# The last tile's stores, one transfer a quadrant instead of two, and another order of the last products, in a linear-attention and mixture-of-experts kernel

## The chip, the cores and the metric

The kernel runs on one core of a Trainium2 chip. The metric is the device time of one execution in microseconds (us); for several runs it is their median. A core has five engines with instruction streams of their own, which wait for each other through semaphores: TensorE (PE, its weight loads are shown as PEld), VectorE (DVE), ScalarE (ACT), GpSimd (POOL) and SyncE (SP). Transfers (DMAs) are issued by SP, ACT or POOL and carried out by 16 DMA engines.

## What is computed

```
x   = linear attention of q, k, v          # 8 batches, 8 heads, 576 positions, 64 wide
x   = x as 4608 tokens of 512              # token = batch * 576 + position
p   = domain_probs / (sum + 1e-9)          # 4608 x 4
out = 0
for e in range(4):                         # four experts
    h = max(x @ w1[e], 0)                  # 512 -> 1024
    out += p[:, e:e+1] * (h @ w2[e])       # 1024 -> 512
```

The output is 4608 x 512 in float32.

## The kernel before

**Tiles.** The tokens are worked on in nine tiles of 512 (`NT`). Tiles 0 to 7 are the first 512 positions of the eight batches. Tile 8, the last, collects the 64 positions that are left over in each batch (512 to 575). A tile has four subtiles `ns` of 128 tokens, one to a partition; in tile 8 a subtile is two batches of 64 positions: batch 2·ns on partitions 0 to 63, batch 2·ns+1 on partitions 64 to 127. In the output these two pieces lie 576 rows apart.

**Products.** For each tile but the first and each expert (a unit, 32 of them) both layers multiply two by two blocks with seven products instead of eight. Layer 1 is done by `Block` in two halves (`d` = 0, 1) and leaves the hidden values `h`; POOL forms four sums of them a half (`hidden_sum`, L776 to L782), each of 128 x 512 elements. Layer 2 (`layer2_product`, L784) has products numbered 1 to 7, each for two token groups `i` = 0, 1. One of them is four matmuls (L809) of 128 x 256 into half a PSUM bank, after which VectorE adds the bank, times p, to the float32 accumulator of the subtile (`add_acc`, L705). Products 1, 6, 7 and 4 run on in one bank half (`run`), so 4 can only start when the accumulation of 7 has read it; 2, 5 and 3 use the other (`side`). A name such as m83.41 is tile 8, expert 3, product 4, group 1. Two units follow each other at the end: m82.* and, behind it, m83.*, the last. In the last unit `run` and `side` are banks of their own (pb, pe) instead of halves of py.

**Order.** The order of work is written by hand. Every piece has a position (a number); `work` is sorted by it (L1100) and then issued one after the other (L1115), which sets the order on every engine. Layer 2's products of a unit stand at `at` + `L2AT[m]`, in the order `L2ORD`, (2, 5, 1, 6, 3, 7, 4); the last unit has an order of its own and stands 7 later (L1075). A piece that yields is driven to its end before the next one begins, so a product, its accumulation and its store are recorded together.

**Stores.** `store` (L683) writes an accumulator to the output. For tiles 0 to 7 that is one transfer on SP of 128 rows of 2,048 bytes (256 KB, L686). For tile 8 it writes only a quadrant at a time, 128 rows of 256 columns (1,024 bytes): two transfers of 64 rows, one per batch, on SP and ACT (L692). Products 2, 3, 4 and 7 each finish a quadrant per group, so there are eight quadrants and 16 transfers of 64 KB. Those of product 7, group 1, are both on POOL (L832). A transfer raises one semaphore when it lands; eight semaphores (lanes) serve SP's and ACT's transfers in turn, and a transfer first waits until the former one of its lane has landed. Behind the last instruction, SP tests the lanes one after the other (L1143), and a barrier of all engines ends the execution.

Of the kernel before, what the change touches and what calls it, by code (L numbers as in the profile page):

```python
# [80 lines left out]
    "KC": ('VV', 'VA', 'AA', 'AV'),  # L81
    "XT": ('AA', 'VV', 'VA', 'VV'),
    "CUT": (((0, 3, 4), (0, 3, 4), (0, 4), (0, 4)), ((0, 2, 4),) * 4),
    "WARM": (14, 5, 3, 1, 2, 1, 1),
    "BANK": {'qT0': 'b', 'qT1': 'py', 'kv2': 'py', 'qT2': 'py', 'kv3': 'b', 'nd10': 'b', 'nd10+': 'py', 'nd00': 'py', 'xT20': 'b', 'nd01': 'b', 'xT00': 'b', 'xT10': 'py', 'xT30': 'py', 'nd11': 'b', 'L20': 'b', 'xT11': 'b', 'L30': 'e', 'L10': 'e', 'L11': 'e', 'L00': 'py', 'L31': 'b', 'L01': 'e', 'L21': 'py', 'b1.lk': 'py', 'b1.q1': 'py', 'b1.q3': 'b', 'b1.q0': 'py', 'b1.nd10': 'b', 'b1.qT0': 'py', 'b1.nd00': 'b', 'b1.xT0': 'b', 'b1.xT3': 'py', 'b1.qTl': 'py', 'b1.nl': 'py'},
    "EARLY": (
# [36 lines left out]
def kernel(  # L123
# [10 lines left out]
    nc = tc.nc  # L134
    ATTN, HSUM, L2ORD, L2AT = (CFG[x] for x in ("ATTN", "HSUM", "L2ORD", "L2AT"))

    B, H, S, D = q.shape
    N, E = moe_domain_probs.shape
    _, Dm, F = moe_w1.shape

    P = 128
    HP = P // 2
    CM = S // P
    SM = CM * P
# [67 lines left out]
    out_b = out.rearrange("(b s) d -> b s d", s=S)  # L212
# [467 lines left out]
    def new_py():  # L680
        return ppm.tile([P, Dm], FP32, tag="py", bufs=2, name="py")

    def store(j, ns, cols=slice(0, Dm), engs=(nc.sync, nc.scalar)):  # L683
        acc = accs[j, ns][:, cols]
        if j < B:
            nc.sync.dma_start(  # L686
                out=out_b[j, 0:SM].rearrange("(p c) d -> c p d", c=CM)[ns],
                in_=acc,
            )
        else:  # L690
            for u in range(2):
                engs[u].dma_start(  # L692
                    out=out_b[2 * ns + u, SM:S, cols],
                    in_=acc[u * HP : (u + 1) * HP],
                )

    def add_acc(j, e, ns, ps, ds, first):
        if (j, ns) not in accs:
            accs[j, ns] = pm.tile([P, Dm], FP32, tag="acc", bufs=NACC, name="acc")
        acc = accs[j, ns][:, ds]  # L700
        pscal = p_sb[:, j, ns, e : e + 1]
        if first:
            nc.scalar.activation(acc, ps, AF.Identity, scale=pscal)  # L703
        else:
            nc.vector.scalar_tensor_tensor(  # L705
                out=acc, in0=ps, scalar=pscal, in1=acc, op0=AO.mult, op1=AO.add
            )
# [61 lines left out]
    def hidden_sum(h, hs, i):  # L769

        a11, a21 = h[:, :, 0, 0:NH], h[:, :, 0, NH:NT]
        a12, a22 = h[:, :, 1, 0:NH], h[:, :, 1, NH:NT]
        if i != 2:
            hs[i] = pm.tile([P, 2, NH], FP16, tag=f"hs{i}", bufs=2, name=f"hs{i}")
        if i == 0:
            nc.gpsimd.tensor_tensor(out=hs[0], in0=a21, in1=a22, op=AO.add)  # L776
        elif i == 1:
            nc.gpsimd.tensor_tensor(out=hs[1], in0=hs[0], in1=a11, op=AO.subtract)  # L778
        elif i == 2:
            nc.gpsimd.tensor_tensor(out=a21, in0=a11, in1=a21, op=AO.subtract)  # L780
        else:
            nc.gpsimd.tensor_tensor(out=hs[3], in0=a12, in1=hs[1], op=AO.subtract)  # L782

    def layer2_product(j, e, hT, hss, p, i):  # L784


        if (j, e) == (NTILES - 1, E - 1):
            if p == 1:
                pys[j, e, i] = [ppm.tile([P, DH], FP32, tag=tag, bufs=2, name=f"p{tag}") for tag in ("b", "e")]
            run, side = pys[j, e, i]  # L790
        else:
            if p == 2:
                pys[j, e, i] = new_py()
            run, side = pys[j, e, i][:, 0:DH], pys[j, e, i][:, DH:Dm]
        ts = slice(i * P, (i + 1) * P)
        ts2 = slice(NH + i * P, NH + (i + 1) * P)
        w, tw = w2_sb[e], t2_sb[e]
        lo, hi = slice(0, FH), slice(FH, FC)
        ps, lhsT, rhs, first = {
            1: (run, lambda k: hT[k // 2][:, k % 2, 0, ts], w[:, lo, 0:DH], (j, e) == (NTILES - 1, E - 1)),  # L800
            2: (side, lambda k: hT[k // 2][:, k % 2, 1, ts], w[:, hi, 0:DH], True),
            5: (side, lambda k: hss[k // 2][0][:, k % 2, ts], tw[:, 0], True),
            6: (run, lambda k: hss[k // 2][1][:, k % 2, ts], tw[:, 1], False),
            7: (run, lambda k: hT[k // 2][:, k % 2, 0, ts2], w[:, lo, DH:Dm], False),
            3: (side, lambda k: hss[k // 2][3][:, k % 2, ts], w[:, hi, DH:Dm], False),
            4: (run, lambda k: hT[k // 2][:, k % 2, 1, ts2], tw[:, 2], False),
        }[p]
        for k in range(FH):
            nc.tensor.matmul(  # L809
                out=ps,  # L810
                lhsT=lhsT(k),
                rhs=rhs[:, k],
                start=first and k == 0,
                stop=k == FH - 1,
                skip_group_check=True,
            )
        yield
        c1, c2 = slice(0, DH), slice(DH, Dm)
        ns, ds, first = {
            2: (i, c1, True),  # L820
            5: (2 + i, c2, True),
            1: (i, c1, False),
            6: (i, c2, True),
            7: (2 + i, c2, False),
            3: (i, c2, False),
            4: (2 + i, c1, True),
        }[p]
        add_acc(j, e, ns, ps, ds, first and e == 0)
        if (j, e) == (NTILES - 1, E - 1):
            if p in (2, 3, 4, 7):  # L830
                yield
                store(j, ns, ds, *([(nc.gpsimd,) * 2] if (p, i) == (7, 1) else ()))  # L832
        elif e == E - 1 and p in (3, 4):
            yield
            store(j, ns)
# [166 lines left out]
    with tc.manual_schedule(  # L1002
# [5 lines left out]
        work = []  # L1008

        def put_at(pos, name, *g):  # L1010
            work.append((pos, len(work), name, g))
# [24 lines left out]
        NSLOT, LAG = 7, 6  # L1036

        def put_block(at, *g):
            bl = Block(*g)
            for pos, name in ((0, "p1"), (3, "p2"), (5, "p6"), (8, "p7"), (9, "p5"), (9.1, "c22"), (11, "p4"), (13, "p3")):  # L1040
                put_at(at + pos, f"{name}.{g[0]}{g[1]}{g[2]}", getattr(bl, name))
# [18 lines left out]
        for n, (j, e) in enumerate(units):  # L1060
            h, hss = [None, None], [[None] * 4, [None] * 4]
            at = base + 2 * NSLOT * n
            for d in range(2):
                put_block(at + d * NSLOT, j, e, d, h)
            at += 2 * NSLOT + LAG

            def hsum(d, i, hT=h, hss=hss):
                hidden_sum(hT[d], hss[d], i)

            for d in range(2):  # L1070
                for i in range(4):
                    put_at(at + HSUM[d][i], f"hs{j}{e}.{d}{i}", hsum, d, i)
            order = L2ORD
            if n == len(units) - 1:
                order, at = (1, 2, 6, 5, 7, 3, 4), at + NSLOT  # L1075
            for m in range(14):
                put_at(at + L2AT[m], f"m{j}{e}.{order[m // 2]}{m % 2}", layer2_product, j, e, h, hss, order[m // 2], m % 2)

        for j in range(0, NTILES - 1):
            at = base + 2 * NSLOT * E * (j - 1) if j else 0.0  # L1080

            def put(pos, *g, at=at):
                put_at(at + pos, *g)

            if j + 1 < B:
                nxt = bts[j + 2] if j + 2 < B else None
                batch_steps(bts[j + 1], nxt, put, ATTN[j > 0], ATTN[1])
            else:
                put(CFG["LATE"][0], "b0.alloc", b0.alloc_left)
                put(CFG["LATE"][0], "b0.load", b0.load_left, "q")  # L1090
                put(CFG["LATE"][1], "b0.lq", b0.left_act, "q")
                put(CFG["LATE"][2], "b0.lqm", b0.left_dve, "q")
                put(CFG["LATE"][2] + 1, "b0.qTl", b0.dma_qTl)
                put(CFG["LATE"][3], "b0.nl", b0.nd_left)
            for i in range(4):
                if j:
                    put(2 * NSLOT * E + CFG["TSUM"][i], f"ts{j + 1}.{i}", token_sum, j + 1, i)
                else:
                    put(base + CFG["TSUM1"][i], f"ts1.{i}", token_sum, 1, i)
        work.sort(key=lambda w: w[0:2])  # L1100
        live = {name: g for _, _, name, g in work}
        assert len(live) == len(work)
# [45 lines left out]
```

## Time and profile before

| | |
|---|---|
| median of three runs | 491.01 us (491.0 to 491.03) |
| the profiled execution | 491.24 us |
| its span, first to last instruction | 489.5 us (489.46) |
| busy: PE | 477.5 us, 98% |
| busy: DVE | 382.2 us, 78% |
| busy: POOL | 358.3 us, 73% |
| busy: ACT | 330.8 us, 68% |
| granted TensorE clock | 0.998 |
| data moved by DMA | 53.67 MB, of which 9.44 MB written to HBM |
| last matmul begins | 484.82 us |
| last accumulation ends | 485.61 us |

Times within the profile are microseconds from the span's start. The profiled execution takes 1.78 us more than its span, and 0.23 us more than the median. The chain of waits is followed back from the last instruction of an engine: each piece in it is either what released the next or the instruction before it on its engine. "PE py L809 x8" are eight matmuls of line 809 into the tile py; "pb" and "pe" are the banks of the last unit. SPq and ACTq are instructions that the sequencers of SP and ACT carry out, such as the issue of a transfer. In the DMA rows q1 is SP's queue, q10 ACT's and q0 POOL's; a row gives packets, megabytes and the share that the packets took of the time of all 16 DMA engines. A packet is one row of a transfer, or the 4 bytes that raise the semaphore.

### The profile page before, as it was taken

What the parts mean: (1) busy time and instruction counts of PE and PEld (TensorE: products, weight loads), DVE (VectorE), ACT (ScalarE), POOL (GpSimd) and SP (SyncE); (2) the same over time, 40 slices, a digit from 0 to 9 for tenths busy, and PEclk for the clock granted to TensorE, in tenths of its full rate; (3) what the DMA queues carried; (4) which work ended last, traced back from release to release, by engine and by line L of the source; (5) the groups of instructions that cost most, each with busy time, mean ns of one, the idle gap of its engine ahead of it and who ended that gap; (6) DMA issues with size and microseconds to landing.
All of it is one profiled execution on the core that took longest, in us unless ns stands there. A gap on an engine that the chain in (4) does not pass through costs nothing.

```text
span 489.5 us, 12007 instructions
## 1 busy us (share of the span) xinstructions
PE 477.5 (98%) x4567; PEld 407.8 (83%) x4567; DVE 382.2 (78%) x801; ACT 330.8 (68%) x656; POOL 358.3 (73%) x341
## 2 busy tenths in 40 slices
PE   7899998999999999999999999999999999999996
PEld 3676665898888988898889888988898888888885
DVE  5768999998958886788769885978687756775686
ACT  5489979855896498748884888478954565446530
POOL 4655044688967896789776976697769877987775
PEclk9999999999999999999999999999999999999999
DMA  8999968532445235524552345423131020002003
GB/s 280 199 226 262 249 127 243 154 94 47 134 154 122 50 112 190 113 60 113 171 128 65 95 144 145 92 56 119 56 76 28 5 95 1 2 0 88 2 1 86
DMA packets 81017, 53.67 MB, mean 110 GB/s; under 512 B 45152, under 2 KB 73696, under 8 KB 80960
## 3 DMA queue, kind: packets, MB, share of 16 engines
q1 hardware_dynamic: 70512, 41.05, 30.7%
q0 software_dynamic: 9888, 11.41, 12.3%
q8 instruction: 35, 0.57, 0.5%
q10 hardware_dynamic: 560, 0.46, 0.3%
q14 instruction: 22, 0.18, 0.1%
HBM read 45.16 MB, written 9.44 MB: 112 GB/s over the span
## 4 chain that ended last, share of the span: by engine, by line
PE 91%; ACT 3%; DVE 2%; DMA 1%; issue 1%; SPq 0%; DVEq 0%; ACTq 0%
PE py L809 39%; PE pb L866 24%; PE pe L866 18%; PE py L714 4%; PE ph L654 1%; PE psum_nd L471 1%; DMA kraws<-in_k_dram 1%; PE psum_kv L443 1%; DVE acc L705 1%; PE pb L809 1%; PE pe L809 0%; DVE t L761 0%; PE psum_nl L489 0%; ACT kp L343 0%; ACT u L877 0%
## 5 line engine op out<-in xcount | busy, mean ns | idle before, releaser
L705 DVE SCALAR_TENSOR_TENSOR acc<-py,p_sb,acc 128x256 f32<-128x256 f32 (+1 forms) x382 | 181.7, 488 | 43.1 <-PE py L809 37.3
L850 DVE CUSTOM_DVE_ANT_0 h<-pe,u 128x512 f16<-128x512 f32 x140 | 96.0, 687 | 46.8 <-PE pe L866 27.1
L866 PEld LDWEIGHTS <-w 128*128 128x128 f16 x1120 | 109.1, 98 | 17.4 <-issue 1.3
L776 POOL TENSOR_TENSOR hs<-h 128x512 f16<-128x512 f16 x64 | 73.9, 1154 | 59.4 <-DVE h L850 57.5
L809 PEld LDWEIGHTS <-h 128*128 128x128 f16 x1024 | 99.6, 98 | 12.7 <-issue 1.2
L809 PE MATMUL py<-w,h 128*128 128x256 f16 x744 | 106.4, 273 | 0.6 <-ACT acc L703 0.6
L877 ACT COPY u<-pb 128x512 f32<-128x512 f32 x140 | 82.5, 592 | 32.4 <-PE pb L866 29.7
L778 POOL TENSOR_TENSOR hs<-hs,h 128x512 f16<-128x512 f16 x64 | 75.0, 1173 | 26.4 <-PE py L809 24.0
L866 PEld LDWEIGHTS <-s 128*128 128x128 f16 x840 | 81.4, 98 | 12.1 <-issue 1.1
L866 PE MATMUL pb<-tt,w 128*128 128x256 f16 x560 | 83.7, 273 | 0.9 <-ACT u L877 0.9
L809 PEld LDWEIGHTS <-hs 128*128 128x128 f16 x768 | 74.4, 98 | 8.9 <-POOL hs L776 0.2
L782 POOL TENSOR_TENSOR hs<-h,hs 128x512 f16<-128x512 f16 x64 | 74.7, 1168 | 0.9 <-PE py L809 0.3
L780 POOL TENSOR_TENSOR h<-h 128x512 f16<-128x512 f16 x64 | 74.8, 1168 | 0.2
L809 PE MATMUL py<-t,hs 128*128 128x256 f16 x496 | 74.3, 273 | 0.0
L899 ACT ACTIVATE h<-pe 128x512 f16<-128x512 f32 x70 | 42.0, 600 | 44.1 <-PE pe L866 40.7
L892 ACT COPY pe<-pb 128x512 f32<-128x512 f32 x70 | 40.1, 574 | 38.6 <-PE pb L866 14.1
L920 ACT ACTIVATE h<-pb 128x512 f16<-128x512 f32 x70 | 42.0, 600 | 7.0 <-PE pb L866 7.0
L866 PE MATMUL pb<-tt,s 128*128 128x256 f16 x280 | 41.8, 272 | 0.6 <-ACT pe L892 0.6
L866 PE MATMUL pe<-tt,s 128*128 128x256 f16 x280 | 41.9, 273 | 0.0
L866 PE MATMUL pe<-xT,s 128*128 128x256 f16 x248 | 37.3, 273 | 0.0
L866 PE MATMUL pe<-xT,w 128*128 128x256 f16 x248 | 37.2, 273 | 0.0
L866 PE MATMUL pb<-xT,w 128*128 128x256 f16 x248 | 37.0, 273 | 0.0
(133 smaller groups left out, 598.7 us busy)
## 6 DMA issues: line engine op xcount, KB each, us to landing
out_dram<-acc SPq DMA_DIRECT2D x32, 256.0 KB, 2.5
w<-in_moe_w_dram POOLq DMA_DIRECT2D x14, 512.0 KB, 10.7
rawb<-in_k_dram SPq DMA_DIRECT2D x24, 256.0 KB, 3.3
rawb<-in_v_dram SPq DMA_DIRECT2D x24, 256.0 KB, 2.8
rawb<-in_q_dram SPq DMA_DIRECT2D x24, 256.0 KB, 2.7
rawq<-in_q_dram SPq DMA_DIRECT2D x4, 256.0 KB, 5.5
w<-in_moe_w_dram POOLq DMA_DIRECT2D x4, 256.0 KB, 6.1
rawb<-in_k_dram POOLq DMA_DIRECT2D x4, 256.0 KB, 8.6
```

The lines of the kernel that those rows point to most:

```text
L705: nc.vector.scalar_tensor_tensor(out=acc, in0=ps, scalar=pscal, in1=acc, op0=AO.mult, op1=AO.add)
L776: nc.gpsimd.tensor_tensor(out=hs[0], in0=a21, in1=a22, op=AO.add)
L778: nc.gpsimd.tensor_tensor(out=hs[1], in0=hs[0], in1=a11, op=AO.subtract)
L780: nc.gpsimd.tensor_tensor(out=a21, in0=a11, in1=a21, op=AO.subtract)
L782: nc.gpsimd.tensor_tensor(out=hs[3], in0=a12, in1=hs[1], op=AO.subtract)
L809: nc.tensor.matmul(out=ps, lhsT=lhsT(k), rhs=rhs[:, k], start=first and k == 0, stop=k == FH - 1, skip_group_check=True,)
L850: nc.vector._custom_dve(TENSOR_ADD_SAT, out=out, in0=ps, in1=u, s0=BIG, s1=0.0)
L866: nc.tensor.matmul(out=ps[:, kk], lhsT=lk(kc), rhs=rhs[:, kc], start=first and kk == 0 and kc == 0, stop=kc == 1, skip_group_check=True,)
L877: nc.scalar.copy(u, self.b)
L892: nc.scalar.copy(self.e5, self.b)
L899: nc.scalar.activation(self.h[:, :, 0, 0:NH], self.e5, AF.Relu)
L920: nc.scalar.activation(self.h[:, :, 1, 0:NH], self.b, AF.Relu)
```

## The change

A quadrant of the last tile goes out by one transfer: the output side covers both batches (2 x 64 rows of 256 columns), the SBUF side all 128 partitions. Group 0's stores are issued by SP, group 1's by ACT; POOL stores nothing any more. In the last unit product 5 comes before product 6. And five products get a fixed position: m83.10, m83.11, m83.20 and m83.21 come to stand directly behind m82.71, before m82.40, and m82.41 between m83.61 and m83.70. TensorE's order from there on is, before, m82.40 .41, m83.10 .11 .20 .21 .60 .61 .50 .51 .70 .71 .30 .31 .40 .41, and after, m83.10 .11 .20 .21, m82.40, m83.50 .51 .60 .61, m82.41, m83.70 .71 .30 .31 .40 .41. VectorE's accumulations follow the same order. Up to m82.71 no engine's order changes.

```diff
     "CUT": (((0, 3, 4), (0, 3, 4), (0, 4), (0, 4)), ((0, 2, 4),) * 4),
+    "MOVE": {"m83.10": 512.0, "m83.11": 512.0, "m83.20": 512.0, "m83.21": 512.0, "m82.41": 528.0},
...
-    def store(j, ns, cols=slice(0, Dm), engs=(nc.sync, nc.scalar)):
+    def store(j, ns, cols=slice(0, Dm), eng=nc.sync):
...
-            for u in range(2):
-                engs[u].dma_start(
-                    out=out_b[2 * ns + u, SM:S, cols],
-                    in_=acc[u * HP : (u + 1) * HP],
-                )
+            eng.dma_start(
+                out=out_b[2 * ns : 2 * ns + 2, SM:S, cols],
+                in_=acc,
+            )
...
-                store(j, ns, ds, *([(nc.gpsimd,) * 2] if (p, i) == (7, 1) else ()))
+                store(j, ns, ds, nc.sync if i == 0 else nc.scalar)
...
-                order, at = (1, 2, 6, 5, 7, 3, 4), at + NSLOT
+                order, at = (1, 2, 5, 6, 7, 3, 4), at + NSLOT
...
+        work = [(CFG["MOVE"].get(w[2], w[0]), *w[1:]) for w in work]
         work.sort(key=lambda w: w[0:2])
```

## The prediction

> **What bounds the kernel now.** I read the chain of waits first, then its last microseconds, the timeline from 477 us on, the rows of the store's line (L692), and the DMA rows by stretch. The page's chain says that TensorE sets the time almost everywhere:
>
> ```profile
> PE 91%; ACT 3%; DVE 2%; DMA 1%; issue 1%; SPq 0%; DVEq 0%; ACTq 0%
> ```
>
> In order of time, from 477 us to the end (start, length, what), the chain has one break and a tail:
>
> ```profile
> 477.50 0.40 DVE acc L705
> 477.90 0.04 issue
> 477.94 1.03 PE py L809 x8
> ...
> 483.38 2.23 DVE acc L705 x5
> ```
>
> The reader is to see two things. PE waits for the accumulation at 477.50 before it starts the last products of the unit before (m82.40, m82.41); it could have gone on at 477.48, since m82.71's last matmul started at 477.37 and matmuls follow each other every 0.109 us. So about 0.46 us of PE is lost. And the work ends at 485.61 with VectorE's last accumulation, 3.85 us ahead of the span's end (489.46). What fills those 3.85 us is the stores:
>
> ```profile
> 484.33 2.39 SPq L692 DMA_DIRECT2D out_dram<-acc  x4
> 484.33 2.69 ACTq L692 DMA_DIRECT2D out_dram<-acc  x4
> 484.69 0.92 DVE L705 SCALAR_TENSOR_TENSOR acc<-pb,p_sb,acc 128x256 f32<-128x256 f32 x2
> ```
>
> The last accumulation ends at 485.61, but both queues issue back to back until 487.02; ACT's last store starts only at 486.47, 0.85 us late, because four stores of some 0.6 us each stand in each queue. The rows of L692 give issue times (min/median/max in ns) and the time to landing:
>
> ```profile
> L692 SPq DMA_DIRECT2D out_dram<-acc x7: 467/547/561, 480.8 to 486.2; - x7
> L692 ACTq DMA_DIRECT2D out_dram<-acc x7: 497/571/810, 480.8 to 486.5; - x7
> ...
> DMA to landing us min/median/max: 1.9/2.2/2.6
> ```
>
> 486.47 + 2.01 to landing = 488.48, and 0.98 us of final waits and barriers (L1143) end the span.
>
> **The change, part by part.** Nothing ahead of 477.4 us moves: the order of every engine's instructions is the same up to m82.71.
>
> (1) Order of products. m83.10 to m83.21 go ahead of m82.40, m82.41 goes behind m83.61, and 5 goes before 6. All operands exist: a12 of the second block was written at 475.94, and the pe bank was free at 477.51. Removed is the break of 0.46 us. In steps of 0.437 us from 477.48, m83.41, the sixteenth product, starts at 484.03 instead of 484.49, so the last accumulation ends at 485.16: a gain of 0.46 us. What is late next: m83.60 needs POOL's sum that ends at 480.53, in its third matmul at 480.75; m83.30 needs POOL's last sum (482.75), in its third matmul at 482.94. Neither stalls, by 0.2 us; if that cover were gone, at most the 0.46 us would come back. VectorE (0.39 us a piece when back to back, 477.51 to 477.90) follows PE's 0.437. The first store becomes ready at 479.48 instead of 480.82.
>
> (2) Removed transfers. 16 stores of 64 KB become 8 of 128 KB, four on SP and four on ACT, none on POOL. The two POOL issues (0.56 us each) are off the end: they landed by 487.14. With one store per quadrant and queue there is no queueing: the last quadrant is ready at 485.16, its queue has been free since about 484.9, so the issue starts at 485.18 instead of 486.47: 1.29 us earlier, of which 0.46 are from (1). No store waits for an earlier one's semaphore any longer, since eight transfers use eight lanes once.
>
> (3) How the new transfers are cut. This is what decides. The SBUF side stays 128 rows of 1,024 bytes, but the DRAM side is now 2 x 64 x 256 elements, two batches 576 rows apart; before, each transfer was 64 x 256 on both sides. In the trace every transfer of this program lands by 16 increments of its semaphore, and a store of 64 rows leaves 64 + 16 packets (560 = 7 x 80 in the rows below): 16 engines with four rows each. But every one of these transfers has an outermost dimension of 64 or 128 on both sides, which 16 divides. None has an outermost 2. If the cut is made on the outermost dimension alone, the new store can only go to two engines, 64 rows each. The price of a row is bounded by two stretches, here 480 to 489.5 us, the stores of 64 rows (packets, MB, share of the 16 engines' time):
>
> ```profile
> q1 hardware_dynamic: 560, 0.46, 20.3%
> q10 hardware_dynamic: 560, 0.46, 17.7%
> ```
>
> and 440 to 446 us, the stores of 128 rows of 2 KB:
>
> ```profile
> q1 hardware_dynamic: 529, 0.99, 44.1%
> ```
>
> The first: 38.0% x 16 x 9.5 us / 896 rows = 64 ns a row, with two queues and all engines busy. The second: 44.1% x 16 x 6 us / 967 KiB = 44 ns per KiB. Of the 23,424 packets of 1,024 bytes in the trace half took 46 ns or less; I take 46, since two engines leave the memories nearly idle, and keep 44 and 64 as ends.
>
> Then with two engines for both queues: 8 stores x 64 rows = 512 rows an engine x 46 ns = 23.6 us. The first packet comes 1.21 us after an issue (480.84 to 482.05), so at 479.50 + 1.21 = 480.71. There is no gap: the first two stores keep the engines busy until 486.6, and by then all eight are issued. The last packet ends at 504.3; its semaphore 0.34 us later (488.14 to 488.48 before); then 0.98 us, and 0.31 us more, because SP tests the lanes in a fixed order, 0.061 us each, and the last store's lane is now followed by six tests instead of one. Span 505.9, that is 16.5 us more. Against the profiled execution (491.24 = 489.46 span + 1.78 around it) this is 507.7; the median of the runs is 0.23 lower, so 507.5. Parts (1) and (2) are then covered: PE and VectorE end at 485.2, 19 us ahead of the last row.
>
> [...]
>
> **The rivals.**
> Rival 1, all 16 engines (the transfer is cut by its rows): the other side, not slower. For it: each store's SBUF side still has 128 rows, and the stores of 128 rows of 2 KB (256 KB) land in 2.2 to 2.5 us. Against it: the 2 on the DRAM side. Issue at 485.18, landing 2.25 us later (bounds 1.94 and 2.58, the extremes of the 64 KB stores) = 487.43, plus 0.98 + 0.31 = 488.72: 0.74 us less, 490.3 (489.9 to 490.6). It decides as soon as more than about twelve engines carry a store. [...]
> Rival 2, two engines for SP's stores and two others for ACT's: 256 rows an engine. ACT's last three stores have rows from 483.43 + 1.21 = 484.64 on and need 3 x 64 x 46 ns = 8.8 us: 493.5; end 495.1, 5.6 us more: 496.7. Against it: in the trace both queues use all 16 engines, so neither owns a set.
> Rival 3, the dear row: two engines at 64 ns. 512 x 65 ns = 33 us: 517. For it: the rows of 480 to 489.5, which are these very stores. Against it: there, 16 engines ran at once.
>
> **How the numbers follow.** Two engines for all (forecast, with rival 3 in its range): 0.82, of which rival 3 has 0.12. Rival 2: 0.04. Rival 1: 0.14, of which 0.03 reach past 490.03. I weigh the outermost dimension so high because it is the only thing in which the new transfers differ in kind from all others of the trace. Slower by over 0.2% (0.98 us, about what a measurement of this kernel can tell from no change): 0.86; within: 0.11; faster: 0.03. The range goes from 500, which allows for packets of the two queues overlapping on an engine, to 518 (64 ns a row, and 0.5 us for part 1): 0.81. It leaves out rivals 1 and 2.
>
> **What would show it.** Right: landings of L692 of many microseconds, growing from store to store; q1 and q10 together at two sixteenths of the engines' time (a DMA share of 0.12) for some 20 us with PE idle; the last accumulation at 485.2 and no break at 477.5. Wrong: landings of 2 to 2.6 us (then rival 1 and 490.3); landings that halve (rival 2). If the last accumulation ends at 485.6 or later, part (1) failed, which here changes nothing of the time.

## The result, and the profile after

The changed kernel takes 507.01 us (506.51 to 507.72, four runs) against 491.01 (491.0 to 491.03, four runs as well): 16.0 us more, ratio 1.0322, 95% interval 1.0304 to 1.034. The profiled execution took 506.98 us, its span is 505.16. The profiled executions here differ by up to 2 us ahead of the last 13 us, where their code is nearly equal: the last add-and-relu (L850) starts at 475.8 to 478.8 us. So below the tails are compared, from the start of that instruction to the span's end. That is 12.65 us before (476.81 to 489.46) and 28.44 us after (476.72 to 505.16): 15.8 us more.

The chain of waits, share of the span by engine, has lost PE share, though no PE work was added:

```profile
PE 87%; ACT 2%; DVE 2%; DMA 2%; issue 1%; SPq 1%; ACTq 0%; DVEq 0%
```

The chain of the changed kernel in order of time, from 476 us on (start, length, what), has no break any more:

```profile
476.69 0.87 PE py L809 x8
477.56 0.87 PE pb L809 x8
478.43 0.87 PE pe L809 x8
479.31 0.44 PE py L809 x4
479.74 0.87 PE pe L809 x8
480.62 0.87 PE pb L809 x8
481.49 0.44 PE py L809 x4
481.93 0.87 PE pb L809 x8
482.80 0.87 PE pe L809 x8
483.67 0.89 PE pb L809 x8
484.56 0.02 issue
484.58 0.48 DVE acc L705
```

PE goes from m82.71 straight to m83.10, and the last accumulation ends at 485.07, 0.54 us earlier than before (0.08 of it from the stretch ahead of the tail). All the engines that compute are then done, 20 us ahead of the end. The timeline of the last stores:

```profile
483.79 5.47 SPq L692 DMA_DIRECT2D out_dram<-acc  x2
...
484.23 6.31 ACTq L692 DMA_DIRECT2D out_dram<-acc  x2
```

and the rows of L692, issue times min/median/max in ns:

```profile
L692 SPq DMA_DIRECT2D out_dram<-acc x4: 512/603/4597, 479.4 to 484.7; - x4
L692 ACTq DMA_DIRECT2D out_dram<-acc x4: 527/1008/5347, 479.9 to 485.2; - x4
```

Where before a median of 2.2 us stood between issue and landing, the trace's semaphore updates now give 5.7, 8.0, 9.6, 10.2, 14.2, 14.7, 18.7 and 18.7 us for the eight stores in order of issue. The DMA rows from 478 to 506 us (0.7 us a digit or number; the digits are tenths of all 16 engines) show why:

```profile
DMA  0000111111111111111111111111111111110000
GB/s 0 0 0 9 26 35 34 48 41 48 47 48 45 50 34 48 48 50 47 50 47 48 48 48 48 48 48 48 48 48 48 48 48 48 48 48 19 0 0 0
...
q1 hardware_dynamic: 520, 0.52, 5.6%
q10 hardware_dynamic: 520, 0.52, 5.4%
```

The reader is to see two things. The DMA share is a flat 1 for 23 us: between one and two tenths of 16 engines, as two engines at work would give (0.125). And the packets count the engines by themselves: each queue wrote 4 x 128 = 512 rows, so 8 of the 520 packets are the ones that raise a semaphore, two a transfer. Before, 560 = 7 x (64 + 16) had sixteen a transfer.

### The profile page after: what moved, and what is told of

The parts are those of the page before. It is cut to its first block, busy times and chain, and to the rows that moved or that the text cites. A ratio compares the mean times of both kernels' runs of the same rounds, so it can differ in the third digit from the quotient of the medians.

```text
span 505.2 us, 11996 instructions
## 1 busy us (share of the span) xinstructions
PE 476.2 (94%) x4567; PEld 407.6 (81%) x4567; DVE 382.2 (76%) x801; ACT 330.8 (65%) x656; POOL 357.2 (71%) x339
## 4 chain that ended last, share of the span: by engine, by line
PE 87%; ACT 2%; DVE 2%; DMA 2%; issue 1%; SPq 1%; ACTq 0%; DVEq 0%
PE py L809 37%; PE pb L866 23%; PE pe L866 17%; PE py L714 4%; PE ph L655 1%; PE psum_nd L472 1%; DMA rawq<-in_q_dram 1%; PE psum_kv L444 1%; DMA out_dram<-acc 1%; PE pb L809 1%; PE pe L809 1%; DVE acc L705 1%; SPq L540 0%; DVE t L761 0%; PE psum_nl L490 0%
## 5 line engine op out<-in xcount | busy, mean ns | idle before, releaser
L850 DVE CUSTOM_DVE_ANT_0 h<-pe,u 128x512 f16<-128x512 f32 x140 | 96.1, 687 | 47.1 <-PE pe L866 24.9
L877 ACT COPY u<-pb 128x512 f32<-128x512 f32 x140 | 82.5, 592 | 32.4 <-PE pb L866 29.6
L892 ACT COPY pe<-pb 128x512 f32<-128x512 f32 x70 | 40.1, 574 | 38.6 <-PE pb L866 14.2
```

What stands on the lines that cost most here:

```text
L850: nc.vector._custom_dve(TENSOR_ADD_SAT, out=out, in0=ps, in1=u, s0=BIG, s1=0.0)
L877: nc.scalar.copy(u, self.b)
L892: nc.scalar.copy(self.e5, self.b)
```

## The experiments

Theory, as forecast: a transfer is cut over the DMA engines by the outermost dimension of its access patterns; 2 on the output side leaves two engines. Rivals: that 128 KB in one transfer, or its two pieces 576 rows apart, are slow in themselves; that the new order of the products costs time.

The ratios are to the kernel before as it was run beside each (medians 491.01 to 491.18 us); a tail is that of the one profiled execution. The kernels rows_first, outer4 and outer8 leave the last tile's rows elsewhere in the output: they are there to tell the causes apart, and no candidates.

| kernel | median us | ratio to before, 95% interval | tail us | semaphore packets a store |
|---|---|---|---|---|
| before | 491.01 | | 12.65 | 16 |
| changed, 2 x 64 rows | 507.01 | 1.0304 to 1.034 | 28.44 | 2 |
| stores_only | 507.95 | 1.0321 to 1.0354 | 29.76 | 2 |
| order_only | 490.76 | 0.9977 to 0.9999 | 12.19 | 16 |
| outer4, 4 x 32 rows | 497.17 | 1.0109 to 1.0136 | 18.42 | 4 |
| outer8, 8 x 16 rows | 492.91 | 1.0022 to 1.0052 | 14.24 | 8 |
| rows_first, 64 x 2 rows | 490.40 | 0.9971 to 0.9994 | 11.74 | 16 |
| pool_more | 492.61 | 1.0019 to 1.0048 | 13.60 | 16 |
| tokens_turned | 519.96 | 1.0567 to 1.06 | 11.75 | 16 |
| turned_write | 514.33 | 1.0451 to 1.05 | 11.75 | 16 |

**order_only**, the order without the new stores: in the changed kernel, `store` and its call are those of before.

```diff
-            eng.dma_start(
-                out=out_b[2 * ns : 2 * ns + 2, SM:S, cols],
-                in_=acc,
-            )
+            for u in range(2):
+                engs[u].dma_start(
+                    out=out_b[2 * ns + u, SM:S, cols],
+                    in_=acc[u * HP : (u + 1) * HP],
+                )
```

> The changed order of the products with the stores of before (two transfers of 64 rows a quadrant). Both theories, the cut by the outermost dimension (two engines) and the size (128 KB in one transfer is slow in itself), put no cost into the order: the gap of 0.46 us on PE ahead of m82.40 goes, every store starts 0.46 us earlier, and the queues end 0.46 us earlier: 490.5 us, 0.5 less than before. A third theory, that the order costs time, gives 491 or more.

Measured: 490.76 us, and the tail is 0.46 us shorter than before, what was expected. The median's 0.25 us says less, since single runs of either kernel spread by about 2 us. The order costs nothing; the third theory falls.

**stores_only**, the kernel before with the new `store` and call.

> The new stores with the old order of the products. Two engines: the first store is issued at 480.84 instead of 479.42 us, and from its first row on 512 rows an engine run without a gap, so everything ends 1.4 us later than in the changed kernel: 508.4 us. If the order had a share in the loss, this kernel would be faster than the changed one's 507.0.

Measured: 507.95 us, 0.45 less than expected, but the tail is 1.32 us longer than that of the changed kernel, near the 1.4 expected. The first store was issued at 480.78 instead of 479.42 us (1.36 later). So the whole loss comes with the stores, and the time is that of a stream that begins with the first store.

**rows_first**, one edit on the changed kernel:

```diff
-                out=out_b[2 * ns : 2 * ns + 2, SM:S, cols],
+                out=out_b[2 * ns : 2 * ns + 2, SM:S, cols].rearrange("u r d -> r u d"),
```

> The changed kernel with one edit: the output side of a last-tile store is walked as 64 x 2 rows instead of 2 x 64. Same bytes, same addresses, same size, queue and number of transfers; the rows of the two batches are written in another order, so the last tile's rows of the output stand elsewhere. Cut by the outermost dimension: 64 lets all 16 engines take part, landings of 2 to 2.6 us, all 16 increments late, 490.3 us (489.9 to 490.6). If the size of 128 KB, the two pieces 576 rows apart, or one transfer a queue were the cause: 507, with landings that grow to 18 us.

Measured: 490.40 us. The rows of L692 and the DMA rows from 478 to 506 us:

```profile
L692 SPq DMA_DIRECT2D out_dram<-acc x4: 539/558/644, 480.4 to 485.7; - x4
L692 ACTq DMA_DIRECT2D out_dram<-acc x4: 546/546/676, 480.9 to 486.1; - x4
...
DMA to landing us min/median/max: 2.1/2.1/2.2
```

```profile
DMA  0000055000798800000000000000000000000000
...
q1 hardware_dynamic: 576, 0.52, 5.6%
```

Here the flat line of ones has become two short bursts; 576 - 512 = 64 semaphore packets for four stores are 16 each. Bytes, addresses, number, size and queues are those of the changed kernel, and the share of engine time (5.6%) is the same: the same work, on 16 engines instead of two. That settles it against the size and against the two pieces: 16.6 us hang on which of two dimensions stands outermost on the output side.

**outer4 and outer8** set the dimension to 4 and 8: `out_b[ns % 2 * 4 : ns % 2 * 4 + 4, SM + ns // 2 * 32 : SM + ns // 2 * 32 + 32, cols]` and `out_b[0:8, SM + ns * 16 : SM + ns * 16 + 16, cols]`.

> The changed kernel with each last-tile store written as 4 x 32 rows (four batches, 32 positions each) instead of 2 x 64; the last tile's rows of the output stand elsewhere. Cut by the outermost dimension: four engines, 32 rows each, 1.43 us a store at the 44.7 ns a row that the changed kernel showed. The last six stores have rows from 484.1 us on and run 8.6 us: the span ends at 494.3, time 496.2 us, and every transfer shows 12 early increments and 4 late ones. Size as cause: 507 as the changed kernel.

> The same with 8 x 16 rows. Eight engines, 16 rows each, 0.72 us a store: the last six stores run from 484.1 to 488.4, the span ends at 490.0, time 491.9 us, with 8 early increments and 8 late ones. Size as cause: 507.

Measured: 497.17 and 492.91 us, each 1.0 us more than expected. The DMA rows from 478 to 506 us of outer4 and then of outer8:

```profile
DMA  0000222212222222222222000000000000000000
...
q1 hardware_dynamic: 528, 0.52, 6.2%
```

```profile
DMA  0002450025555551000000000000000000000000
...
q1 hardware_dynamic: 544, 0.52, 6.2%
```

528 and 544 are 4 and 8 semaphore packets a store; the level of the DMA share, 2 and 5 tenths, goes with 4/16 and 8/16. Of the missing microsecond, 0.7 us is in the span of the profiled execution, where the stream of rows ended later than forecast: a packet took 51 to 52 ns on average, against 48 in the changed kernel (the median is 46 in all three). Why, no run shows.

**pool_more**, from order_only, an attempt to shorten the queues:

```diff
-                store(j, ns, ds, *([(nc.gpsimd,) * 2] if (p, i) == (7, 1) else ()))
+                store(j, ns, ds, *([(nc.gpsimd,) * 2] if (p, i) in ((7, 1), (3, 1)) else ()))
```

> The new order of the products and two transfers of 64 rows a quadrant as before, but the quadrant of product 3, group 1, also on POOL, so that SP and ACT issue three stores each behind 483.8 us instead of four. The last store on ACT then starts at about 485.4 instead of 486.0: 490.2 us (490.0 to 490.5). If POOL's own transfers (0.56 us each to issue, landed 2.4 us later) become the last: 490.5, as with the order alone.

Missed: 492.61 us, slower than before. ACT's last store did start 0.21 us after the last accumulation, as planned, but it landed after 3.1 us instead of 2.0, and the end waits for POOL now. The chain ends there, and of the DRAIN instructions that the engines run behind their last work (count, ns min/median/max) POOL's is the longest:

```profile
486.22 1.08 POOL out_dram L693 x2
487.29 0.52 POOLq L1145
```

```profile
L1145 POOLq DRAIN  x3: 46/93/4543, 487.0 to 492.1; - x3
```

Begun at 487.05, it ends at 491.59, 3.8 us after POOL's last issue and 0.9 us after SP reached the barrier (490.73). In the kernel before the same drain (4.06 us, begun at 484.60) ended at 488.66, 0.02 us ahead of SP: POOL's transfers were close to being the bound there too. The profiled execution was one of the longer ones (494.14 us; twelve runs took 491.49 to 494.5), so how much of the median's loss is POOL's drain stays open.

**tokens_turned and turned_write** try to keep the fast stores with the whole output in place. From rows_first, the last tile's tokens are put on the partitions in the order in which the rows are walked, by a view in layer 1's `products` (and the load of the probabilities likewise). In tokens_turned the matmul reads in that order, in pairs of tokens that lie 64 elements apart; the main lines of the edit:

```diff
-                out=t[u * HP : (u + 1) * HP, B],
+                out=t[u:P:2, B],
...
+                turn = [lambda a, o=o: a.rearrange(o, i=2, u=2) for o in ("p (i r u) -> p i r u", "p (i u r) -> p i r u")]
...
-                        out=ps[:, kk],
+                        out=turn[0](ps[:, kk]),
                         lhsT=lk(kc),
-                        rhs=rhs[:, kc],
+                        rhs=turn[1](rhs[:, kc]),
```

In turned_write the matmul writes in that order instead: the two patterns are `"p (i r u) -> p i u r"` and `"p (i u r) -> p i u r"`.

> The stores of rows_first, and the last tile's tokens put in the same order on the partitions, so that the whole output is the reference's: in that tile's layer 1 the moving operand is read with a step of 64 elements, and the probabilities are loaded to every second partition. Two engines as cause: 490.3 us if TensorE reads such an operand at full rate; each ns that a matmul loses costs 0.22 us in the tile's 224 such matmuls, so half rate (0.109 us each lost) gives 515. Size as cause: 507 or more.

> As tokens_turned (stores walked as 64 x 2 rows, the whole output the reference's), but the last tile's tokens are turned where layer 1's matmuls write: the moving operand is read straight, the PSUM output is written with a step of two elements. If only the reading with a step cost tokens_turned its 29.6 us, the tail is that of rows_first: 490.4 us, 0.6 less than before. If TensorE also pays for a write with a step: 0.22 us for each ns that one of the 224 matmuls loses, 520 at the same 132 ns.

Measured: 519.96 and 514.33 us. The costliest PE groups of tokens_turned from 470 us on, and of turned_write likewise (busy us, mean ns of one):

```profile
L869 PE MATMUL pb<-tt,w 128*128 128x256 f16 x32 | 9.1, 405 | 0.0
L809 PE MATMUL py<-w,h 128*128 128x256 f16 x56 | 7.7, 272 | 0.0
```

```profile
L869 PE MATMUL pb<-tt,w 128*128 128x256 f16 x31 | 8.1, 413 | 0.0
```

A turned matmul of 256 columns took 404 to 416 ns in these views, the others 272 to 283. These durations overlap (in the kernel before, matmuls of 272 ns start every 0.109 us), so the cost is read from the times: 29.6 us over rows_first / 224 matmuls is 132 ns each for the read with a step; 23.9 / 224 = 107 ns for the write. The tails of both, 11.75 us, are that of rows_first, so the loss lies ahead of the stores. Both cost far more than the 0.6 us they could save.

So of the kernels that put every row in its place, order_only is the fastest: the old two transfers a quadrant and the new order, 490.76 us.

## Why the prediction was right

- **Part 1, the order.** Forecast: the break goes, which is worth 0.46 us, hidden behind the stores. From the last L850 to the end of the last accumulation 8.804 us became 8.346: 0.46. order_only's tail shows that it is worth just that when the stores do not hide it. POOL's sums came in time.
- **Part 2, fewer issues.** The queueing ahead of the last store went: in the changed kernel its issue began at 485.19 (forecast 485.18), in rows_first 0.03 us after the last accumulation (486.07, 486.11). The tail of rows_first is 0.91 us shorter than before; rival 1's sum was 0.74, the difference being a landing in 2.08 us instead of the 2.25 put in.
- **Part 3, the cut.** This decided. Two engines, for both queues alike: from 488 to 502 us each queue has 333 packets and 6.8%, together 13.6%, two sixteenths and a little; where only one queue has work it goes twice as fast (12 rows in 0.25 us, against 6 and 6). So rival 2 is out: SP's and ACT's stores share the two engines. A store's semaphore shows it as well: that of the first has three updates, one 1.05 us after the issue began, ahead of the first packet (1.27 us), and two at 5.68 and 5.74. In the kernel before, that of the first store has sixteen, the first 1.78 us after the issue began (first packet 1.21 us). The trace does not give the size of an update, so the early increments that the expectations count (12, 8 and none) are the author's estimate. The semaphore packets a store, 2, 4, 8 and 16 for 2, 4, 8 and 64 on the output side, go with the theory. That the new stores would use two engines, and both queues the same two, was an estimate when it was put into the sum: in the kernel before every store left sixteen such packets, so no run had shown it.
- **The price of a row.** 512 rows were put in at 46 ns, 23.6 us, on the author's estimate that two engines load the memories little (the stream moved about 48 GB/s, the stores of before up to 328); the stream took 22.9 us (480.69 to 503.55), 44.7 ns a row. That this came so near is in part luck, for two errors had opposite signs. The prediction saw no gap in the stream, but its first rows were slow: up to 482.7 us the packets took 70 ns on average (the first GB/s above, 26 to 35). Later the packets took the 46 ns put in but overlapped a little on the two busy engines, which is why two sixteenths read 13.6% instead of 12.5%: from 488 to 502 us 658 rows passed, 42.6 ns a row on each engine. Why the first were slow is not shown. Rival 3's 64 ns was the price with all engines busy, and did not apply; it counted the semaphore packets in, the rows of that stretch alone took 62 ns.
- **The issues.** The prediction had all eight stores issued by 486.6. The last two issues ended at 489.3 and 490.5 instead (last section); the two engines had rows to write all the same.
- **The end.** Last packet to landing 0.33 us (0.34 put in), landing to the span's end 1.285 (0.98 + 0.31 = 1.29). The order of SP's tests is real: six tests of 0.061 us follow the last store's lane.
- **The sum.** 16.5 us forecast, 15.8 in the tail and 16.0 between the medians; 507.5 against 507.01. The term of the sum that was off is the stream, by 0.7 us.
- **One transfer in place of two.** What it was worth hung on the output side: with the same order of the products, two transfers a quadrant took 490.76 us (order_only), one with 64 x 2 rows 490.40, one with 2 x 64 rows 507.01.

## What to carry to other kernels

Before joining transfers, look at the outermost dimension of the output side: here it, not the size, set how many DMA engines worked, and the packet count tells it (128 rows and 2, 4, 8 or 16 small packets a store, for 2, 4, 8 or 64). Only the output side was varied; the SBUF side had 128 rows throughout. A stretch with a flat, low DMA share and idle engines at the end of a kernel is worth that check first. And an order that frees the last instruction gains nothing while something slower ends behind it; the two parts of such a change are best timed apart.

## What the runs showed of the hardware that was not expected

- The issue of a transfer can itself be held up: SP's and ACT's last stores took 4.6 and 5.3 us to issue in the changed kernel, with three stores of 64 rows an engine issued ahead of each on the same queue. In stores_only ACT's third store was held up too (2.6 us, its fourth 5.2); with 4 x 32 rows the last stores took 0.5 and 0.8 us. It cost nothing here. What sets the point at which it begins was not tried.
- POOL's drain behind its last transfer lasts: it ended 3.4 us after the last issue before, 3.4 in order_only and 3.8 in pool_more, later than that transfer's landing (2.4 to 2.7 us after its issue began).
- Matmuls of 256 columns took 405 ns instead of 273 when the moving operand was read in pairs 64 elements apart, and about 410 when the output was written with a step of two elements; in time each cost 132 and 107 ns.
